# Modulation row 0 behind a third w2^T block, later sines behind the first norm, and the first MLP block among the last w2^T blocks

## The chip, the cores and the metric

The kernel runs on one core of a Trainium2 chip. The core has TensorE (PE in the profile; its weight loads are listed apart as PEld), VectorE (DVE), ScalarE (ACT), GpSimd (POOL) and SyncE (SP), which issues most of the DMA transfers. The metric is the device time of one execution in microseconds. Every number is a time on the chip or a line of a profile taken there.

## The reference, cut to what matters

The computation is one transformer-like block, forward and backward, in bf16: S = 2048 tokens, D = 1024 channels, F = 3584 hidden units. Six modulation rows come from one vector c.

```python
def _A_ref(x, w_r, w_i):                       # spectral filter over tokens and channels
    X = rfft2(x.astype(float32))
    return irfft2(X * (w_r + 1j * w_i), s=(S, D)).astype(bfloat16)

def _B_ref(x, w1, b1, w2, b2):                 # MLP with a norm of its own
    h = gelu(layernorm(x) @ w1 + b1)           # tanh approximation
    return h @ w2 + b2

mod = (silu(c) @ w_mod).reshape(1, 6, 1, 1024)
sa, ca, ga, sb, cb, gb = mod rows 0 .. 5
h = layernorm(x) * (1 + ca) + sa
x = x + ga * _A_ref(h, A_w_r, A_w_i)
h = layernorm(x) * (1 + cb) + sb
x = x + gb * _B_ref(h, B_w1, B_b1, B_w2, B_b2)
# returned: x, and the gradients of the weighted output with respect to
# A_x, A_w_r, A_w_i, B_w1, B_b1, B_w2, B_b2, c and w_mod, for a given grad_out
```

## The kernel before, in words

Tokens go in four chunks of 512 (index i, b or j), hidden units in 28 blocks of 128 (fc), modulation rows in halves of 512 columns. The Fourier transforms are matrix products with sine and cosine matrices that the kernel makes itself. The program is laid out at build time: a scheduler puts the instructions into one fixed list for each engine, by priority and by dependencies. Besides the data, three kinds of calls order it: `ordered()` chains matmuls behind the last one, `issue_after(x)` places what follows behind x in a list, and `behind(a, b)` places one instruction behind another. On the chip each engine works through its own list in order, and so does the queue of SP.

The parts that the change touches come in this order:

- **Start.** `start_load` issues the first transfers on SP, one behind the other: modulation weights (`w`), blocks of w2 transposed by the DMA (`t`, `load_w2t`, L344), chunks of grad_out (`g`) and of x (`x`). `mod_block(r, h)` computes half h of modulation row r in 8 matmuls (L280, out to `rows`, `sar` and others at L283). `pt_part` transposes grad_out (L386). `ph_part(fc, js)` computes block fc of ph = w2^T times the transposed gradient, 8 matmuls for each token chunk j (L371), copies the result out on DVE or ACT (L377) and stores it to `d_ph` (L379). `wt`, the tile for w2^T, holds two blocks `fg`, each of two fc, so a new block can only be loaded when the block two before it is used up.
- **Sine matrices.** `gen_mats` calls `trig` ten times. Each call makes index products on POOL (L460), masks them on DVE (L487) and takes the sine on ACT (L488). Calls 1 to 6 fill the matrices `smA` and `smB` of the token transform; calls 7 to 10 give `em`, the small matrices of the channel transform, which ACT then scales (L513) and POOL stores (`d_E`, L516).
- **Norm and fold of x.** For each chunk, statistics (`ln_dve` on DVE at L538 to L549, or `ln_mix`, half on DVE and half as squares on ACT, L548 to L556), a square root on ACT (L528), the normalisation on ACT (`norm_act`, L563), and then the scaling by 1 + row 1 and the even and odd parts over tokens and channels on DVE (`fold_tok`, `fold_d`, `fold_pair`; all recorded at L196, tile `fbuf`). Row 0 is folded alone (`sar`, `saf`) and added at the end.
- **Spectral core.** Its first matmuls are pu (L586 and L580), followed by pcs (L625), pv (L695, L711) and po (L793). Free `ph_part` matmuls (L371) stand between and behind them. `consume_fwd` takes each chunk of the result on DVE and ACT: unfolding, residual, two norms, and the store of the normed chunk `d_n3` (L898, called `d_n` in the profile).
- **MLP.** `load_w1` loads the seven blocks of w1 (L912). `z_block(b, g)` loads its part of ph (L964), computes z for token chunk b and w1 block g in 32 matmuls (pz, L970), and evaluates gelu and its derivative on ACT (L973, L980, L984, L986) and DVE. Before the first block of a chunk the normed chunk is loaded transposed (`n3Ta`, `n3Tb`, L955). `bo_pass` computes the output (pbo, L1027). `plan` is the written-out order of z blocks, remaining ph parts and output passes. The backward pass follows.

In `plan` the first z block stands ahead of the remaining halves of the last four ph blocks:

```python
plan = [("z", 0, 0)] + [("p", fc, 0) for fc in range(PH_KEEP, NFC)] + [("z", 0, 1), ("z", 0, 2), ("z", 0, 3)]
```

ACT evaluates sine, square root and sigmoid from tables, and loads another table (ACT_TABLE_LOAD) when its list goes from one to another.

Of the kernel before, what the change touches and what calls it, by code (L numbers as in the profile page):

```python
# [23 lines left out]
NFC = F // P  # L24
# [11 lines left out]
def kernel(  # L36
# [390 lines left out]
    for what in (("w", 5, 0), ("t", 0), ("w", 5, 1), ("g", 0), ("g", 1), ("x", 0), ("g", 2), ("g", 3),  # L427
                 ("w", 1, 0), ("w", 1, 1), ("x", 1), ("t", 1), ("x", 2), ("x", 3)):
        start_load(*what)
    for step in ((mod_block, 5, 0), (mod_block, 5, 1), (pt_part, 0, range(4), held), (gb_turn,), (pt_part, 0, range(4, 8)),  # L430
                 (pt_part, 1, range(4)), (ph_part, 0, (0,)), (pt_part, 1, range(4, 8)), (ph_part, 1, (0,)),
                 (pt_part, 2, range(4)), (ph_part, 0, (1,)), (pt_part, 2, range(4, 8)), (ph_part, 1, (1,)),
                 (pt_part, 3, range(4)), (ph_part, 0, (2,)), (pt_part, 3, range(4, 8)), (ph_part, 1, (2,)),
                 (mod_block, 1, 0), (mod_block, 1, 1), (ph_part, 0, (3,)), (ph_part, 1, (3,))):
# [42 lines left out]
    gcount = [0]  # L477

    def trig(dst, colv, rowv, nrow, width, modn, cosine):
# [3 lines left out]
        for r in range(nrow):  # L483
# [3 lines left out]
        nc.vector.tensor_scalar(out=idx[:, 0:n], in0=idx[:, 0:n], scalar1=modn - 1, scalar2=None, op0=ALU.bitwise_and)  # L487
        nc.scalar.activation(out=dst, in_=idx[:, 0:n].rearrange("p (r w) -> p r w", w=width), func=ACT.Sin,  # L488
                             bias=negpi[:], scale=2 * np.pi / modn)
# [341 lines left out]
    for h in range(2):  # L831
        mod_block(0, h)
# [17 lines left out]
    load_w2t(2)  # L850
    for fc in range(2, PH_EARLY):
        ph_part(fc, (0, 1, 2, 3))
        if fc % 2 == 1:
            load_w2t(fc // 2 + 2)
            if fc > 3:
                with tc.issue_after(last_pe[0].ins):
                    for r, h in late_mods[3 * (fc // 2 - 2):3 * (fc // 2 - 1)]:
                        mod_block(r, h)

    scaled = []  # L860
    for i in range(4):
        x4, fb = x4s[i], fbuf[:, i]
        if i == 0:
            with tc.issue_after(ev_v[1, 2].ins), tc.issue_after(ev_a[1, 7].ins):
                ln_dve(x4, 0, i)
                norm_act(fb, x4, 0, i)
        else:
            with tc.issue_after(ev_v[3, 6].ins if i == 1 else scaled[i - 2].ins), tc.issue_after(ev_a[3, 7].ins):
# [5 lines left out]
        if i % 2 == 0:  # L874
            fold_d(fb, fb, x4[:])
# [40 lines left out]
    for fc in range(PH_EARLY, NFC):  # L916
        if fc % 2 == 0 and fc > PH_EARLY + 2:
            load_w2t(fc // 2)
            load_w1((0, 2, 1, 4)[max(fc // 2 - 10, 0)])
        ph_part(fc, (0, 1, 2, 3) if fc < PH_KEEP else (0, 1))  # L920
# [30 lines left out]
    def z_block(b, g0, g1):  # L951
        n3T = n3Ts[b % 2]
        if g0 == 0:
            with tc.issue_after(w2ts[11].ins) if b == 0 else ExitStack():
                n3_in = nc.sync.dma_start_transpose(out=n3T[:], in_=d_n3[b * BW:(b + 1) * BW, :])  # L955
            if b == 0:
                for ins in w1_in[:2]:
                    behind(ins, n3_in)
        for g in range(g0, g1):
# [3 lines left out]
            with tc.issue_after(w2t_in[0].ins) if n < 2 else ExitStack():  # L963
                nc.sync.dma_start(out=ph, in_=d_ph_v[:, g * 4:(g + 1) * 4, b * BW:(b + 1) * BW])  # L964
# [98 lines left out]
    plan = [("z", 0, 0)] + [("p", fc, 0) for fc in range(PH_KEEP, NFC)] + [("z", 0, 1), ("z", 0, 2), ("z", 0, 3)]  # L1063
# [7 lines left out]
    for kind, b, g in plan:  # L1071
        if kind == "z":
            z_block(b, g, g + 1)
        elif kind == "p":
# [509 lines left out]
```

## Time and profile before

| | |
|---|---|
| runs | 1439.34, 1443.11, 1444.62 us; median 1443.11 |
| profiled execution | 1442.74 us, of which the span is 1441.0 |
| PE busy | 1382.4 us, 96% of the span |
| DVE busy | 1071.3 us, 74% |
| ACT busy | 743.2 us, 52% |
| POOL busy | 372.5 us, 26% |
| memory traffic | read 166.77 MB, written 115.92 MB, 196 GB/s over the span |

The page also cuts the span into 40 slices of 36 us. Each digit is the busy share in tenths; the third line is the clock that TensorE was granted, in tenths of full speed, and the last the share of the DMA engines:

```profile
PE   6799999979989999999999999999999999999998
DVE  5598889949889787787711588999488658998633
PEclk9799999989999999999999999999999999999999
DMA  9961564898877687697999479986689998667994
```

Slices 1 and 2 are the start with the modulation rows, slice 4 the end of the fold of x, slice 9 the change from the w2^T blocks to the MLP. A row of a timeline gives the start, the duration, the engine, the line, the instruction with its tiles and shapes, the number of instructions taken together, and in brackets the idle time of the engine before it and what ended that. A row of the waits gives microseconds in total, times, and the longest. In a row of windows the busy time of PE, PEld, DVE, ACT and POOL stands with the number of instructions, followed by the granted clock, the share of the DMA engines and GB/s.

### The profile page before, as it was taken

The numbers are of one execution on the slowest core, as the hardware profiler recorded it, in microseconds if no ns is written. First come the engines' busy times: TensorE is split into PE (matmuls) and PEld (weight loads), VectorE is DVE, ScalarE is ACT, GpSimd is POOL, SyncE is SP. The second block draws the span as 40 slices with busy tenths as digits, with TensorE's granted clock in tenths as the row PEclk, the third lists the DMA queues.
The fourth block names the chain that finished last, engine by engine and source line by source line (L and its number), as shares of the span: only waits on it lengthen the run. The fifth ranks groups of instructions, "written<-read, shape, count | busy, mean of one in ns | idle before, by whom it ended". The sixth has DMA issues, their size and how long they took to land. (4 is left out here: it accounts for less than half of the span.)

```text
span 1441.0 us, 18701 instructions
## 1 busy us (share of the span) xinstructions
PE 1382.4 (96%) x6963; PEld 664.6 (46%) x6963; DVE 1071.3 (74%) x1506; ACT 743.2 (52%) x1059; POOL 372.5 (26%) x479
## 2 busy tenths in 40 slices
PE   6799999979989999999999999999999999999998
PEld 3244566434434444444444444444544565444443
DVE  5598889949889787787711588999488658998633
ACT  5575667645887765666413583243532444433211
POOL 6210452400212122122211011112356431322323
PEclk9799999989999999999999999999999999999999
DMA  9961564898877687697999479986689998667994
GB/s 338 295 208 64 150 216 138 229 297 287 252 238 254 220 252 242 203 265 257 254 307 264 129 210 307 280 246 189 222 261 286 246 203 232 188 177 185 281 221 154
DMA packets 356689, 333.22 MB, mean 231 GB/s; under 512 B 207578, under 2 KB 297200, under 8 KB 356470
## 3 DMA queue, kind: packets, MB, share of 16 engines
q1 hardware_dynamic: 319110, 205.61, 54.6%
q0 software_dynamic: 37488, 126.42, 25.1%
q8 instruction: 54, 0.88, 0.3%
q14 instruction: 37, 0.30, 0.1%
HBM read 166.77 MB, written 115.92 MB: 196 GB/s over the span
## 5 line engine op out<-in xcount | busy, mean ns | idle before, releaser
L371 PE MATMUL pp<-gBoT,wt 128*128 128x512 bf16 x896 | 204.9, 388 | 13.4 <-DMA wt<-in_B_w_dram 8.4
L1127 PE MATMUL pg<-w1T,gzr 128*128 128x512 bf16 x896 | 196.1, 379 | 2.6 <-ACT gn3b L1142 1.7
L1478 PE MATMUL gw1acc<-gzh,n3n 128*128 128x512 bf16 x896 | 195.2, 379 | 0.6 <-DVE gwo L1267 0.6
L371 PEld LDWEIGHTS <-wt 128*128 128x128 bf16 x896 | 89.0, 100 | 120.9 <-issue 15.0
L970 PEld LDWEIGHTS <-w 128*128 128x128 bf16 x896 | 87.7, 98 | 112.2 <-issue 9.0
L1127 PEld LDWEIGHTS <-gzr 128*128 128x128 bf16 x896 | 86.5, 98 | 110.7 <-issue 7.9
L1478 PEld LDWEIGHTS <-n3n 128*128 128x128 bf16 x896 | 87.5, 98 | 104.9 <-issue 1.3
L970 PE MATMUL pz<-n3Ta,w 128*128 128x512 bf16 x448 | 100.5, 384 | 5.0 <-ACT gt L973 5.0
L970 PE MATMUL pz<-n3Tb,w 128*128 128x512 bf16 x448 | 99.0, 379 | 0.0
L196 DVE TENSOR_TENSOR ct<-ct 128x2048 bf16<-128x2048 bf16 x68 | 81.0, 1219 | 17.3 <-DMA d_n<-ct 16.3
L973 ACT ACTIVATE gt<-pz,b_col 128x512 bf16<-128x512 f32 x112 | 73.3, 684 | 38.9 <-PE pz L970 38.5
L1027 PEld LDWEIGHTS <-hhA 128*128 128x128 bf16 x608 | 59.0, 98 | 72.3 <-issue 2.1
L1260 PE MATMUL gw2acc<-gB,hhsA 128*128 128x512 bf16 x416 | 91.9, 379 | 0.0
L1482 ACT CAST gwo<-gw1acc 128x512 bf16<-128x512 f32 x49 | 28.6, 583 | 109.9 <-PE gw1acc L1478 102.8
L196 DVE TENSOR_TENSOR gt<-gt,gt 128x2048 bf16<-128x2048 bf16 x56 | 68.5, 1223 | 20.7 <-ACT gt L986 19.6
L984 ACT ACTIVATE gt<-gt 128x2048 bf16<-128x2048 bf16 x28 | 53.4, 1909 | 56.4 <-DVE gt L196 56.4
L1267 ACT CAST gwo<-gw2acc 128x512 bf16<-128x512 f32 x46 | 26.5, 583 | 97.3 <-PE gw2acc L1260 82.8
L377 ACT CAST pho<-pp 128x512 bf16<-128x512 f32 x53 | 30.6, 580 | 66.8 <-PE pp L371 66.7
L1260 PEld LDWEIGHTS <-hhsA 128*128 128x128 bf16 x416 | 40.7, 98 | 47.8
L980 ACT ACTIVATE gt<-gt 128x2048 bf16<-128x2048 bf16 x28 | 53.5, 1910 | 1.5 <-DVE w2sA L196 0.8
L1483 POOL DMA_DIRECT2D out_dram<-gwo x56 | 30.7, 549 | 90.3 <-ACT gwo L1482 54.1
L986 ACT ACTIVATE gt<-gt 128x2048 bf16<-128x2048 bf16 x28 | 53.4, 1909 | 0.4
(345 smaller groups left out, 2544.3 us busy)
## 6 DMA issues: line engine op xcount, KB each, us to landing
gzr<-d_gz SPq DMA_DIRECT2D x28, 512.0 KB, 6.4
wblk<-in_w_mod_dram SPq DMA_DIRECT2D x12, 1024.0 KB, 6.7
out_dram<-otl POOLq DMA_DIRECT2D x48, 256.0 KB, 4.4
out_dram<-gwo POOLq DMA_DIRECT2D x96, 128.0 KB, 4.2
d_ph<-pho POOLq DMA_DIRECT2D x21, 512.0 KB, 4.9
d_hh<-hhA POOLq DMA_DIRECT2D x19, 512.0 KB, 5.0
w<-in_B_w_dram SPq DMA_DIRECT2D x7, 1024.0 KB, 6.1
hhC<-d_ph SPq DMA_DIRECT2D x14, 512.0 KB, 3.5
```

The source lines that it names most:

```text
L196: return nc.vector.tensor_tensor(out=out, in0=a, in1=b, op=op)
L371: last_pe[0] = nc.tensor.matmul(pp[:], lhsT=wt[:, fg % 2, cch, k * P:(k + 1) * P], rhs=gBoT[j][:, cch, :], start=(cch == 0), stop=(cch == ...
L970: last_pe[0] = nc.tensor.matmul(pz[:], lhsT=w1s[g][:, cch, k * P:(k + 1) * P], rhs=n3T[:, cch, :], start=(cch == 0), stop=(cch == NDC - 1))
L973: z_in = nc.scalar.activation(out=zb[:, k, :], in_=pz[:], func=ACT.Identity, bias=b1_col[:, fc:fc + 1], scale=1.0)
L980: nc.scalar.activation(out=av, in_=zb, func=ACT.Square)
L984: nc.scalar.activation(out=sg, in_=bv, func=ACT.Sigmoid, scale=2.0 * GK)
L986: nc.scalar.activation(out=bv, in_=bv, func=ACT.Sigmoid, scale=-2.0 * GK)
L1027: last_pe[0] = nc.tensor.matmul(pbs[i][:], lhsT=hh[:, k, i * P:(i + 1) * P], rhs=wp[:, k, :], start=False, stop=(g == 6 and k == 3))
L1127: last_pg[0] = nc.tensor.matmul(pgs[i][:], lhsT=gzs[b, g][:, k, i * P:(i + 1) * P], rhs=w1Ts[g][:, k, h * KH:(h + 1) * KH], start=(g == 0 ...
L1260: nc.tensor.matmul(acc[:], lhsT=hh_of(fc)[:, t, :], rhs=gBs[t // 4][:, t % 4, h * KH:(h + 1) * KH], start=(t == 0), stop=(t == NT - 1))
L1478: nc.tensor.matmul(acc[:], lhsT=n3ns[t // 4][:, t % 4, cch * P:(cch + 1) * P], rhs=gz2[t // 8][:, t % 8, :], start=(t == 0), stop=(t == NT ...
L1483: nc.gpsimd.dma_start(out=out_4[cch * P:(cch + 1) * P, fg * 512:(fg + 1) * 512], in_=ob)
```

## The change

The change moves work and leaves the arithmetic alone.

1. At the start, x2 is loaded ahead of w2^T block 1. Both halves of row 0 are loaded through `start_load` and computed in the chained order, behind `ph_part(2)`, and w2^T block 2 is loaded behind them. Row 1 is computed ahead of the last five transposes of grad_out's fourth chunk. The late modulation rows are also placed behind the load of block 2.
2. From the fifth `trig` call on, the masks are placed behind the last copy of grad_out's transposes, and the sines behind the norm of x0. From the seventh call on, the masks also go behind the fold of x0. The statistics of x1 to x3 wait for x0's norm in the list, rather than for an earlier copy on ACT.
3. The w1 loads are spread as 0, 1, 1, 5 over the last four `load_w2t` calls in place of 0, 2, 1, 4. Only the first of them is placed behind the load of n3Ta; those from the third on are placed behind the first load of ph.
4. The loop over ph blocks ends at fc 25, and the first halves of fc 26 and 27 come behind the first z block (kind "q" in `plan`).

```diff
-                 ("w", 1, 0), ("w", 1, 1), ("x", 1), ("t", 1), ("x", 2), ("x", 3)):
+                 ("w", 1, 0), ("w", 1, 1), ("x", 1), ("x", 2), ("t", 1), ("x", 3)):
         start_load(*what)
...
-                 (pt_part, 3, range(4)), (ph_part, 0, (2,)), (pt_part, 3, range(4, 8)), (ph_part, 1, (2,)),
-                 (mod_block, 1, 0), (mod_block, 1, 1), (ph_part, 0, (3,)), (ph_part, 1, (3,))):
+                 (pt_part, 3, range(4)), (ph_part, 0, (2,)), (mod_block, 1, 0), (mod_block, 1, 1),
+                 (pt_part, 3, range(4, 8)), (ph_part, 1, (2,)), (ph_part, 0, (3,)), (ph_part, 1, (3,)),
+                 (ph_part, 2, (0, 1, 2, 3))):
...
-        nc.vector.tensor_scalar(out=idx[:, 0:n], in0=idx[:, 0:n], scalar1=modn - 1, scalar2=None, op0=ALU.bitwise_and)
-        nc.scalar.activation(out=dst, in_=idx[:, 0:n].rearrange("p (r w) -> p r w", w=width), func=ACT.Sin,
-                             bias=negpi[:], scale=2 * np.pi / modn)
+        late = gcount[0] > 4
+        with tc.issue_after(ev_v[3, 6].ins) if late else ExitStack():
+            masked = nc.vector.tensor_scalar(out=idx[:, 0:n], in0=idx[:, 0:n], scalar1=modn - 1, scalar2=None, op0=ALU.bitwise_and)
+        if gcount[0] > 6:
+            late_masks.append(masked)
+        sine = nc.scalar.activation(out=dst, in_=idx[:, 0:n].rearrange("p (r w) -> p r w", w=width), func=ACT.Sin,
+                                    bias=negpi[:], scale=2 * np.pi / modn)
+        if late:
+            late_sines.append(sine)
...
     for h in range(2):
-        mod_block(0, h)
+        start_load("w", 0, h)
+        with ordered():
+            last_pe[0] = mod_block(0, h, wm[0, h][:])
+    start_load("t", 2)
...
-    load_w2t(2)
-    for fc in range(2, PH_EARLY):
+    for fc in range(3, PH_EARLY):
         ph_part(fc, (0, 1, 2, 3))
...
-                with tc.issue_after(last_pe[0].ins):
+                with tc.issue_after(last_pe[0].ins), tc.issue_after(w2ts[2].ins):
...
                 norm_act(fb, x4, 0, i)
+            for ins in late_sines:
+                behind(ins, norm_in[0][3])
+            x0_norm = norm_in[0][3]
         else:
-            with tc.issue_after(ev_v[3, 6].ins if i == 1 else scaled[i - 2].ins), tc.issue_after(ev_a[3, 7].ins):
+            with tc.issue_after(ev_v[3, 6].ins if i == 1 else scaled[i - 2].ins), tc.issue_after(x0_norm.ins):
...
-            fold_d(fb, fb, x4[:])
+            folded = fold_d(fb, fb, x4[:])
+            for ins in late_masks if i == 0 else ():
+                behind(ins, folded)
...
-            load_w1((0, 2, 1, 4)[max(fc // 2 - 10, 0)])
-        ph_part(fc, (0, 1, 2, 3) if fc < PH_KEEP else (0, 1))
+            load_w1((0, 1, 1, 5)[max(fc // 2 - 10, 0)])
+        if fc < NFC - 2:
+            ph_part(fc, (0, 1, 2, 3) if fc < PH_KEEP else (0, 1))
...
-                for ins in w1_in[:2]:
-                    behind(ins, n3_in)
+                behind(w1_in[0], n3_in)
...
-                nc.sync.dma_start(out=ph, in_=d_ph_v[:, g * 4:(g + 1) * 4, b * BW:(b + 1) * BW])
+                ph_in = nc.sync.dma_start(out=ph, in_=d_ph_v[:, g * 4:(g + 1) * 4, b * BW:(b + 1) * BW])
+            for ins in w1_in[2:] if n == 0 else ():
+                behind(ins, ph_in)
...
-    plan = [("z", 0, 0)] + [("p", fc, 0) for fc in range(PH_KEEP, NFC)] + [("z", 0, 1), ("z", 0, 2), ("z", 0, 3)]
+    plan = [("z", 0, 0)] + [("q", fc, 0) for fc in range(NFC - 2, NFC)] + [("p", fc, 0) for fc in range(PH_KEEP, NFC)] + [("z", 0, 1), ("z", 0, 2), ("z", 0, 3)]
...
+        elif kind == "q":
+            with ordered():
+                ph_part(b, (0, 1))
```

2 lines of the change are left out of this document (1 added, 1 removed).

## The prediction

> **What bounds the kernel now.** I read the page's head first, then TensorE's waits, then its timeline with the queues beside it.
>
> ```profile
> span 1441.0 us, 18701 instructions
> PE 1382.4 (96%) x6963; PEld 664.6 (46%) x6963; DVE 1071.3 (74%) x1506; ACT 743.2 (52%) x1059; POOL 372.5 (26%) x479
> ```
>
> TensorE (PE) works 96% of the span, so 58.6 us in all can be won by taking waits away. The waits list, TensorE only (what waited, for what; us in total, times, longest), says which of them are large:
>
> ```profile
> PE pm L280 <- DMA wblk<-in_w_mod_dram: 14.8, 4, 4.4
> PE pp L371 <- DMA wt<-in_B_w_dram: 8.4, 1, 8.4
> ```
>
> Both sit where the change works. The timeline of TensorE (start, duration, instruction, count, idle time before it with its releaser) places them:
>
> ```profile
> 43.44 3.62 PE L280 MATMUL pm<-wblk,u_b 128*128 128x512 bf16 x16
> 46.89 3.62 PE L371 MATMUL pp<-gBoT,wt 128*128 128x512 bf16 x16
> 54.96 3.60 PE L280 MATMUL pm<-wblk,u_b 128*128 128x512 bf16 x8 [4.45 <-DMA wblk<-in_w_mod_dram]
> 62.54 3.59 PE L280 MATMUL pm<-wblk,u_b 128*128 128x512 bf16 x8 [3.98 <-DMA wblk<-in_w_mod_dram]
> ...
> 134.32 0.83 PE L586 MATMUL pu<-smA,fbuf 128*128 128x256 bf16 x6 [2.30 <-DVE fbuf L196]
> ...
> 234.58 75.49 PE L371 MATMUL pp<-gBoT,wt 128*128 128x512 bf16 x349
> 318.44 3.59 PE L371 MATMUL pp<-gBoT,wt 128*128 128x512 bf16 x8 [8.38 <-DMA wt<-in_B_w_dram]
> 325.98 14.25 PE L371 MATMUL pp<-gBoT,wt 128*128 128x512 bf16 x56 [3.94 <-DVE phr L377]
> ...
> 411.43 8.75 PE L970 MATMUL pz<-n3Ta,w 128*128 128x512 bf16 x32 [4.58 <-ACT gt L973]
> ```
>
> Three places: the two halves of modulation row 0 (4.45 + 3.98 us, and each half takes 3.6 us for 8 matmuls where 16 took 3.62); the fold of x before the spectral work (2.30); the change-over to the MLP (8.38 + 3.94, later 4.58). By stretches (length, then busy us and count of PE, PEld, DVE, ACT, POOL; granted clock; DMA share; GB/s):
>
> ```profile
> 55.00:59.00 4.00, 3.56 (x8) 0.99 (x8) 0.41 (x1) 3.85 (x8) 0.00 (x0) 0.50 1.04 420
> 59.00:63.00 4.00, 0.46 (x2) 0.19 (x3) 0.28 (x1) 0.00 (x0) 0.00 (x0) 0.50 1.04 389
> ...
> 300.00:311.00 11.00, 10.07 (x47) 4.35 (x45) 3.16 (x8) 10.32 (x12) 1.07 (x2) 1.00 1.17 301
> ...
> 340.00:411.00 71.00, 66.43 (x310) 29.76 (x308) 58.76 (x77) 60.87 (x62) 12.13 (x15) 1.00 0.72 236
> ```
>
> The slow matmuls stand at a granted clock of 0.50 behind a wait of about 4 us. The Trainium skill, page "TensorE: Matmul & The Clock Gate", says in its part on the clock gate that an idle array falls back to half clock; these rows agree.
>
> **The change, part by part.**
>
> *Row 0 behind a third w2^T block.* Thirty-two matmuls of L371 (w2^T block fc 2) move ahead of row 0: 32 x 3.62/16 = 7.2 us of work into the 8.4 us of waits. The second half of row 0 is not earlier by itself; it can only gain what leaves its way. The 1 MB store of the inverse matrices does:
>
> ```profile
> 52.05 0.57 POOL L516 DMA_DIRECT2D d_E<-em  x1 [0.30 <-POOL em L515]
> ```
>
> It now follows later sines. At 389 GB/s 1.05 MB is 2.7 us, so that half starts between 59.9 and 62.5; I take 60.5, and half clock again after a wait of some 3 us. Row 0 then ends near 64.1 rather than 66.1, with 7 us of matmuls already done: TensorE is 9 to 9.5 us ahead. The block needs its own transfer, now behind x2:
>
> ```profile
> 29.78 10.50 SPq L344 DMA_TRANSPOSE wt<-in_B_w_dram  x1
> 40.32 1.95 SPq L143 DMA_DIRECT2D x<-in_A_x_dram  x2
> ...
> 300.91 14.17 SPq L344 DMA_TRANSPOSE wt<-in_B_w_dram  x1
> ```
>
> It is issued 1.95 us later on SP's queue. The block issued at 300.91 took 17.5 us to its use at 318.44, and I know of none slower; 31.7 + 17.5 = 49.2, before TensorE is through at 50.5. So nothing, up to 2.5 us if x2's half megabyte stretches it.
>
> *Sines behind the first norm of x.* ACT and DVE, timelines and (third row) ACT's groups by form:
>
> ```profile
> 46.59 1.28 ACT L528 ACT_TABLE_LOAD   x1
> 47.89 0.30 ACT L528 ACTIVATE mv<-mv,eps_c 128x4 f32<-128x4 f32 x1
> ...
> 70.61 0.59 ACT L377 CAST pho<-pp 128x512 bf16<-128x512 f32 x1 [11.76 <-PE pp L371]
> ...
> 82.77 1.24 ACT L563 ACTIVATE fbuf<-x,stats 128x1024 bf16<-128x1024 bf16 x1
> ```
> ```profile
> L488 ACT ACTIVATE em<-gidx,negpi 128x512 bf16<-128x512 int32 x4 | 2.8, 714 | 0.5 <-DVE gidx L487 0.5
> ```
> ```profile
> 84.10 2.28 DVE L196 TENSOR_TENSOR fbuf<-fbuf,rows 128x4096 bf16<-128x4096 bf16 x1
> 86.30 0.69 DVE L548 BATCH_NORM_STATS2 st<-x 128x6 f32<-128x512 bf16 x1
> ...
> 133.57 0.69 DVE L196 TENSOR_TENSOR fbuf<-fbuf,sb_saf 128x1024 bf16<-128x1024 bf16 x1
> ...
> 324.09 1.23 DVE L196 TENSOR_TENSOR ct<-ct 128x2048 bf16<-128x2048 bf16 x1 [16.31 <-DMA d_n<-ct]
> ```
>
> x0 is scaled and folded early, but the end of the fold (134.26) hangs on x1: its norm ends at 84.0, its scaling starts at 84.10, and 50.2 us of DVE work for x1 to x3 follow with little idle time. After the change the four em sines (2.8 us) and two further table loads (sqrt, sine, sqrt in place of one: 2 x 1.28) stand ahead of x1's norm on ACT, and on DVE a small copy that waits for row 0's matmuls holds the em masks and x1's statistics. ACT's hole of 11.76 us covers most of that: I follow the chain to 84.8, and the fold's end to +1 us (call it d). From below, -1: part of x2's statistics (0.69 us each, as at 86.30) can be done in DVE's free time before x1. From above, +2.5: both loads and half the sines uncovered. Without the hole it would be 2.8 + 2.6 = 5.4, near +6.
>
> In TensorE's order as built 49 more matmuls of L371 stand ahead of the first spectral matmul that needs the fold. 49 x 0.226 = 11 us against 9.5 won: TensorE arrives there as before and waits 2 to 3 us, as before 2.30. So the win is not time yet: it is 46 to 49 finished matmuls, taken from the run of 349 at 234.58. That run would be through some 10 us earlier, and then TensorE waits for the next w2^T block.
>
> *The MLP's start.* So the transfers decide. SP's queue (the row of 300.91, shown above, belongs at the first gap), and the issues of 1 MB (KB each, us to landing) in the same stretch:
>
> ```profile
> 273.29 0.40 SPq L898 DMA_DIRECT2D d_n<-ct  x1
> 282.47 3.09 SPq L344 DMA_TRANSPOSE wt<-in_B_w_dram  x1
> 285.66 13.84 SPq L955 DMA_TRANSPOSE n3Ta<-d_n  x1
> 299.69 1.13 SPq L912 DMA_DIRECT2D w<-in_B_w_dram  x2
> ...
> 315.27 0.44 SPq L912 DMA_DIRECT2D w<-in_B_w_dram  x1
> 315.80 1.34 SPq L898 DMA_DIRECT2D d_n<-ct  x1
> ```
> ```profile
> w<-in_B_w_dram SPq DMA_DIRECT2D x6, 1024.0 KB, 6.1
> ...
> d_x<-xt POOLq DMA_DIRECT2D x2, 1024.0 KB, 7.4
> ```
>
> The block issued at 282.47 waited for TensorE to free its buffer, and the transpose n3Ta stood behind it in the queue. With TensorE 46 x 75.49/349 = 9.9 us ahead, less d, that block goes out right behind the store of the first normed chunk (273.29), and n3Ta waits only for that store: 6.1 to 7.4 us, 279.4 to 280.7. That is 5.0 to 6.3 us earlier than 285.66; I take 5.6. Zero is the other end, if transposes are limited by their transfer and not by their issue. One w1 block less stands ahead of the next w2^T block: 0.56 us of issue and, at 301 GB/s, 1.05 MB = 3.5 us of transfer. So that block, and the second normed chunk's store behind it, come 5.6 + 0.56 + 3.5 - d (1.0) = 8.7 us earlier. The three w1 blocks that now follow a load of ph cost nothing as long as they are used tens of us later; each 1 MB that came late would show as a wait of up to 6.1 us at its block.
>
> Who uses this: DVE waits 16.31 us for that store and frees at 324.09; ACT's and DVE's gelu work then sets the pace to 411.43. TensorE, if it alone decided, has 92.99 - 3.94 - 4.58 = 84.5 us of work from 318.44 to 411.43: from 309.7 it would be there at 394.2 and would wait. So the end of the lead-in moves by DVE's 8.7 us. The 3.94 us wait of TensorE goes with it and is no gain of its own. Against it: the first MLP block now comes among the last w2^T blocks, and ACT, between sqrt and gelu's sigmoid, gets two more table loads, 2 x 1.28 = 2.6 us. ACT is idle 71.00 - 60.87 = 10.1 us of that stretch; so 0 to 2.6, I take 1.3. From the first output matmuls on, the order is the old one.
>
> The Trainium skill, page "ScalarE: Activation LUTs", section "What ACT_TABLE_LOAD costs", adds a drain of about 1.38 us to a load of 1.28. The rows at 46.59 and 47.89 agree on the load and show no drain: the square root starts 0.02 us behind it.
>
> *Sum:* -8.7 + 1.3 = -7.4 us on the profiled execution's 1442.74 (span 1441.0 and 1.74 around it): 1435.3. The median of the runs, 1443.11, lies 0.4 us above that execution. No change is within 0.5%, 7.2 us: 1435.9 to 1450.3.
>
> **The rivals.**
>
> *B, more.* The waits at the MLP's start fall away wholly, ACT's 10.1 us absorb the loads, the fold is 1 us early: -6.3 - 0.56 - 3.5 - 1 = -11.4 and some of the 4.58 us: 1429. For it: TensorE has the 84.5 us of work ready. Against: DVE and ACT are 83 to 86% busy there.
>
> *C, given back.* The fold of x comes some 5 us later than I take it, or n3Ta is no earlier because transposes are bound by transfer: -3.5 - 0.56 + 1.0 + 1.3 = -1.8, or -8.7 + 5 + 1.3 = -2.4: 1440.5. This is also the rival that the change does nothing: row 0's wait turns into one for the fold. For it: a block takes 17.5 us from issue to use, far more than its issue.
>
> *By the page's table switch.* Two switches of 2.66 us, none of it covered: -8.7 + 5.3 = -3.4, 1439.3. In terms of this kernel it is an ACT that loses 2.6 us twice between gelu pieces while TensorE waits on it at L970. Only the loads themselves are in the rows.
>
> *D, slower.* In the new order DVE evacuates the first tile of that next w2^T block before the unfolding that now waits 16.31 us. If the block lands no earlier than 318.44, DVE begins its unfolding where it did, behind an evacuation, and the first MLP block's gelu work (four evacuations, three passes of ACT, seven of DVE) is pushed in front of the second chunk's norms. Then +2.6 to 5.2 us from ACT, and a wait for the last w2^T block before the rest: 1446 to 1452, say 1449. It decides from where the block lands 3 us or more after 318.44. For it: n3Ta and two w2^T blocks in flight at once at a DMA share of 1.17.
>
> **How the numbers follow.** A, as summed, 0.46, own range 1430 to 1439 (0.33 of it faster); B 0.13; C 0.20; the page's switch 0.04; D 0.17. Faster 0.33 + 0.13 = 0.46; within 0.5%, 0.13 + 0.20 + 0.04 = 0.37; slower 0.17. The range leaves out half of D and a third of B: 1428 to 1448.
>
> **What the profile of the changed kernel would show.** Row 0: no wait of 4.45 us, L371 x32 before it, one wait near 3 us. The fold: first needed L586 matmul at 134 to 137, with a wait of 2 to 3 us. The long L371 run: about 303 matmuls rather than 349 before the wait. SP: n3Ta near 280, the next w2^T block near 296. DVE's unfolding free near 315.4 rather than 324.09. The gelu wait at L970 near 404 where it was 411.43, then equal distances to the end. The prediction is wrong if the fold ends past 138, if the wait for wt ends at 318 again, or if ACT's waits at L970 grow by over 5 us.

## The result, and the profile after

The changed kernel takes 1453.51 us (median of 16 runs, 1443.69 to 1466.49) against 1443.03 us for the kernel before (16 runs): a ratio of 1.0084, 95% interval 1.0056 to 1.0112. It is slower by some 10.5 us, where 7.4 us faster was forecast. Its times spread over 23 us, more than those of the kernel before (1432.44 to 1449.73); why is part of the answer. The profiled execution took 1464.85 us, at the slow end. Its page and its list of TensorE's waits:

```profile
span 1463.1 us, 18570 instructions
PE 1372.6 (94%) x6838; PEld 662.9 (45%) x6963; DVE 1071.9 (73%) x1503; ACT 750.9 (51%) x1066; POOL 370.7 (25%) x479
```
```profile
PE pp L371 <- DMA wt<-in_B_w_dram: 40.3, 3, 20.0
PE pz L986 <- ACT gt L989: 12.2, 4, 6.0
PE pm L280 <- DMA wblk<-in_w_mod_dram: 6.5, 3, 3.9
```

The waits for the modulation weights have more than halved (14.8 before), as meant. The waits for w2^T blocks went from 8.4 to 40.3 us. TensorE's timeline tells where (start, duration, instruction, count, idle time before it and its releaser):

```profile
44.04 12.25 PE L371 MATMUL pp<-gBoT,wt 128*128 128x512 bf16 x55 [0.56 <-DVE gBoT L396]
56.12 1.89 PE L280 MATMUL pm<-wblk,u_b 128*128 128x512 bf16 x8
58.34 1.89 PE L280 MATMUL pm<-wblk,u_b 128*128 128x512 bf16 x7 [0.32 <-DMA wblk<-in_w_mod_dram]
...
68.74 13.99 PE L371 MATMUL pp<-gBoT,wt 128*128 128x512 bf16 x62 [1.13 <-DMA wt<-in_B_w_dram]
...
107.86 16.43 PE L371 MATMUL pp<-gBoT,wt 128*128 128x512 bf16 x63 [19.96 <-DMA wt<-in_B_w_dram]
...
153.59 0.83 PE L593 MATMUL pu<-smA,fbuf 128*128 128x256 bf16 x6 [0.95 <-DVE fbuf L196]
...
253.02 65.34 PE L371 MATMUL pp<-gBoT,wt 128*128 128x512 bf16 x296
337.55 9.03 PE L371 MATMUL pp<-gBoT,wt 128*128 128x512 bf16 x32 [19.19 <-DMA wt<-in_B_w_dram]
```

Row 0 is through at 60.2 us (66.1 before). Then two waits of about 20 us stand where there was none and where there was one of 8.38. The first is for w2^T block 3 (fc 6 and 7): the fold of x, first needed at 134.32 before, is first needed at 153.59. DVE's timeline shows how a wait for w2^T gets into the fold:

```profile
90.02 1.21 DVE L196 TENSOR_TENSOR x<-fbuf 128x2048 bf16<-128x2048 bf16 x1
111.49 0.69 DVE L377 CAST pho<-pp 128x512 bf16<-128x512 f32 x1 [20.27 <-PE pp L371]
112.10 1.22 DVE L196 TENSOR_TENSOR x<-fbuf 128x2048 bf16<-128x2048 bf16 x1
```

The copy of block 3's first result out of PSUM (L377) stands in DVE's list in the middle of the fold of x1 (L196). DVE works its list in order, so it stands still for 20.27 us with fold work behind it that lacks nothing. The windows of that stretch, after and then before (length; busy us and count of PE, PEld, DVE, ACT, POOL; granted clock, DMA share, GB/s):

```profile
82.00:88.00 6.00, 5.85 (x27) 2.46 (x26) 6.00 (x7) 3.28 (x8) 0.53 (x1) 1.00 0.83 60
88.00:108.00 20.00, 0.14 (x1) 0.13 (x2) 3.23 (x5) 4.03 (x4) 0.00 (x0) 0.61 1.16 146
```
```profile
88.00:108.00 20.00, 20.00 (x95) 9.05 (x93) 19.88 (x33) 14.18 (x22) 1.07 (x2) 1.00 0.70 226
```

From 88 on TensorE stands still and DVE and ACT have little to do. The DMA engines are busier than before (1.16 against 0.70), and they move less: 60 GB/s in the 6 us ahead of the hole, then 146 against 226. What was in flight, from the queues of SP and POOL:

```profile
57.44 11.36 SPq L272 DMA_DIRECT2D wblk<-in_w_mod_dram  x3
70.80 2.18 SPq L612 DMA_DIRECT2D ws<-in_A_w_r_dram  x1
...
74.51 30.67 SPq L344 DMA_TRANSPOSE wt<-in_B_w_dram  x2
...
292.13 0.40 SPq L912 DMA_DIRECT2D d_n<-ct  x1
292.64 5.11 SPq L344 DMA_TRANSPOSE wt<-in_B_w_dram  x1
297.86 22.26 SPq L970 DMA_TRANSPOSE n3Ta<-d_n  x1
320.34 1.17 SPq L926 DMA_DIRECT2D w<-in_B_w_dram  x1
321.60 13.89 SPq L344 DMA_TRANSPOSE wt<-in_B_w_dram  x1
```
```profile
77.90 0.63 POOL L523 DMA_DIRECT2D d_E<-em  x1 [0.30 <-POOL em L522]
```

Ahead of block 3 (issued at 74.51) stand three late modulation weights of 1 MB each, and 3.4 us behind it, on POOL's queue, the 1 MB store of the inverse matrices (d_E), which the later sines brought there from 52.05. From issue to use block 3 took 107.86 - 74.51 = 33.35 us.

### The profile page after: what moved, and what is told of

The parts are those of the page before. It is cut to its first block, busy times and chain, and to the rows that moved or that the text cites. A ratio compares the mean times of both kernels' runs of the same rounds, so it can differ in the third digit from the quotient of the medians.

```text
span 1463.1 us, 18570 instructions
## 1 busy us (share of the span) xinstructions
PE 1372.6 (94%) x6838; PEld 662.9 (45%) x6963; DVE 1071.9 (73%) x1503; ACT 750.9 (51%) x1066; POOL 370.7 (25%) x479
## 5 line engine op out<-in xcount | busy, mean ns | idle before, releaser
L371 PE MATMUL pp<-gBoT,wt 128*128 128x512 bf16 x873 | 201.1, 386 | 44.9 <-DMA wt<-in_B_w_dram 40.3
L1501 ACT CAST gwo<-gw1acc 128x512 bf16<-128x512 f32 x49 | 28.6, 583 | 110.4 <-PE gw1acc L1497 99.9
L196 DVE TENSOR_TENSOR ct<-ct 128x2048 bf16<-128x2048 bf16 x68 | 81.0, 1217 | 4.2 <-DMA d_n<-ct 3.2
L196 DVE TENSOR_TENSOR gt<-gt,gt 128x2048 bf16<-128x2048 bf16 x56 | 68.4, 1224 | 16.1 <-ACT gt L1002 14.9
L377 ACT CAST pho<-pp 128x512 bf16<-128x512 f32 x61 | 35.2, 587 | 80.2 <-PE pp L371 78.5
```

Of the source, the lines that this page charges most:

```text
L196: return nc.vector.tensor_tensor(out=out, in0=a, in1=b, op=op)
L371: last_pe[0] = nc.tensor.matmul(pp[:], lhsT=wt[:, fg % 2, cch, k * P:(k + 1) * P], rhs=gBoT[j][:, cch, :], start=(cch == 0), stop=(cch == ...
```

## The experiments

The runs of one letter, and e1 with f1 and f2, were measured together with the kernel before. Each ratio is to the kernel before of its own group; between groups the ratios can be compared, the times in microseconds only roughly (the kernel before has medians of 1441.1 to 1443.5). Two tables hold what was read from the profiles, one execution each; the runs follow.

*Block 3.* Queue mark: how long SP took to issue the first ws load. I read 0.35 us as room in SP's queue, and more as a queue in which the loads ahead are not through yet. Then the issue of block 3, the issue of the d_E store, TensorE's first use of the block and its wait, and the first needed pu matmul (for b3 the end of the fold). In b4 and c2 block 3's matmuls stand in one unbroken run with the others. In b1, b2 and e1 row 0 ended late (65.9 to 68.0), which moves the fold by itself.

| run | queue mark | block 3 | d_E | use | wait | fold needed |
|---|---|---|---|---|---|---|
| after | 2.18 | 74.51 | 77.90 | 107.86 | 19.96 | 153.59 |
| a1 | 1.83 | 71.28 | 75.03 | 97.02 | 11.82 | 142.58 |
| c1 | 1.58 | 68.46 | 72.03 | 95.53 | 10.54 | 141.75 |
| b1 | 0.35 | 74.45 | 79.27 | 92.06 | none | 140.28 |
| b2 | 0.35 | 76.61 | 81.43 | 104.42 | none for wt | 148.04 |
| a2 | 1.74 | 69.38 | 73.20 | 103.14 | 18.18 | 148.90 |
| a4 | 1.64 | 82.27 | 51.81 | 102.80 | 5.02 | 143.65 |
| b3 | 1.88 | 69.65 | 73.35 | 102.00 | 16.94 | 129.70 |
| f2 | 1.75 | 69.48 | 73.30 | 96.78 | 11.55 | 142.62 |
| d1 | 0.35 | 67.34 | 72.14 | 87.39 | 2.28 | 132.47 |
| d2 | 1.27 | 68.58 | 101.86 | 86.44 | 1.03 | 131.77 |
| e1 | 0.35 | 75.19 | 108.21 | 92.80 | none | 140.69 |
| b4 | 0.35 | 67.76 | 72.58 | in the run | none | 135.17 |
| c2 | 0.35 | 67.52 | 72.31 | in the run | none | 134.83 |
| before | 0.35 | 80.96 | 52.05 | 99.76 | none | 134.32 |
| f1 | 0.35 | 76.34 | 79.09 | 95.14 | none | 129.69 |
| d3 | 0.35 | 77.14 | 50.86 | 95.94 | none | 130.51 |

*The whole time in four pieces.* Start of the long run of w2^T matmuls; from there to the moment DVE begins to unfold the second chunk; from there to the first matmul on n3Tb; the rest.

| run | run starts | to DVE's unfolding | to n3Tb | rest | span |
|---|---|---|---|---|---|
| before | 234.58 | 89.5 | 99.4 | 1017.5 | 1441.0 |
| after | 253.02 | 92.1 | 102.9 | 1015.2 | 1463.1 |
| a1 | 241.86 | 90.5 | 102.4 | 1015.3 | 1450.0 |
| a2 | 248.03 | 94.1 | 99.2 | 1013.5 | 1454.7 |
| a3 | 234.96 | 89.1 | 99.5 | 1015.4 | 1439.0 |
| c3 | 236.05 | 84.9 | 99.8 | 1014.7 | 1435.5 |
| c4 | 232.53 | 91.9 | 100.1 | 1014.1 | 1438.6 |
| b4 | 233.71 | 90.5 | 102.4 | 1015.6 | 1442.3 |
| c2 | 233.36 | 88.6 | 101.5 | 1013.6 | 1437.0 |
| d2 | 230.96 | 87.8 | 102.7 | 1013.1 | 1434.5 |
| e1 | 239.83 | 83.2 | 103.7 | 1013.6 | 1440.4 |
| f1 | 230.51 | 88.4 | 99.9 | 1017.1 | 1435.9 |
| d3 | 230.87 | 81.5 | 99.4 | 1014.3 | 1426.1 |

### The two halves of the change, and the sines

a1 is the changed kernel again. a2 keeps parts 1 and 2 and undoes the lead-in of the MLP (the w1 spread, the order behind ph, the kind "q"); a3 is the reverse; a4 undoes part 2 alone.

```diff
 a2
-            load_w1((0, 1, 1, 5)[max(fc // 2 - 10, 0)])
+            load_w1((0, 2, 1, 4)[max(fc // 2 - 10, 0)])
 ...
-    plan = [("z", 0, 0)] + [("q", fc, 0) for fc in range(NFC - 2, NFC)] + ...
+    plan = [("z", 0, 0)] + ...
 a4
-        late = gcount[0] > 4
 ...
-            for ins in late_sines:
-                behind(ins, norm_in[0][3])
```

> The changed kernel once more, as the base of the others. Theory L (the w2^T block for fc 6 and 7 lands late; behind its first matmuls stand copies out of PSUM in DVE's and ACT's lists, ahead of the fold of x): TensorE waits at L371 for wt near 90 to 108, by 8 to 20 us, DVE and ACT have a hole of nearly the same length, the first needed L593 matmul comes 6 to 19 us after 134.3, and the time varies with that wait. Rival S (the sines and table loads behind the first norm make the fold late): a late fold without a DVE hole behind a PE release. Time 1449 to 1465 by both.

> The start of the changed kernel (its parts 1 and 2) with the old MLP lead-in (parts 3 and 4 undone). Theory L: the wait for wt near 90 to 108 stays, and nearly all of the loss: 1448 to 1455, ratio to before 1.004 to 1.009. Rival M (the first z block among the w2^T blocks and two more table loads are the loss): 1436 to 1444, ratio 0.995 to 1.001.

> The old start with the new MLP lead-in (parts 3 and 4 alone). Theory L: within 4 us of before, 1439 to 1447, since TensorE isn't ahead there and the two table loads are covered or nearly. Rival M: 1449 to 1455, and waits at L970/L986 for ACT grow by 8 us or more.

> The changed kernel with its part 2 undone: sines, masks and statistics as before, row 0 behind the third w2^T block and the new MLP lead-in kept. SP's order of transfers is that of the changed kernel. Theory L: the wait for wt of 8 to 20 us stays, 1448 to 1456. Rival S: the wait or the hole of DVE goes, 1436 to 1444; the store of the inverse matrices is early again, so if it was what delayed the block, the wait falls below 4 us.

Measured: a1 1456.45 us (ratio 1.0107, 1.0081 to 1.0132); a2 1458.27 (1.0134, 1.009 to 1.0177); a3 1436.52 (0.996, 0.9928 to 0.9991); a4 1450.16 (1.0043, 1.0018 to 1.0067). The start carries the whole loss, and the lead-in alone is faster (a2 came out slower than either of its expected ranges, a3 faster); a3's and c3's profiles do not agree on where (c3 has it ahead of DVE's unfolding, a3 in the rest). a1's profile has the same stall in a smaller size; DVE's hole and TensorE's wait again go together:

```profile
97.02 16.26 PE L371 MATMUL pp<-gBoT,wt 128*128 128x512 bf16 x64 [11.82 <-DMA wt<-in_B_w_dram]
...
142.58 0.83 PE L593 MATMUL pu<-smA,fbuf 128*128 128x256 bf16 x6 [0.95 <-DVE fbuf L196]
```
```profile
100.66 0.69 DVE L377 CAST pho<-pp 128x512 bf16<-128x512 f32 x1 [10.84 <-PE pp L371]
```

In a4 the store is back at 51.81, now beside block 2, and it is block 2 that is late: issued at 50.17, used at 75.83, 25.7 us, with a wait of 6.71. Block 2 had the 2 MB of row 0's loads ahead of it and the store 1.64 us behind it. Block 3 then goes out at 82.27, with a full queue but no store beside it, and takes 20.5 us, of which TensorE waits 5.02; the fold is late (143.65) by holes of 9.53 and 6.65 us in DVE's list, one for each block.

### Does the wait cost through TensorE, or through the lists behind it?

b3 places block 3's copies out of PSUM behind the fold of x in their lists. b1, and c1 with the same kernel, were meant to hold block 4 back from block 3; the edit ordered instructions of different engines, which changed no engine's list, so both are further executions of the changed kernel. b2 places the last three late modulation weights behind block 3.

```diff
 b3
-                nc.any.tensor_copy(out=ov, in_=pv)
+                cp = nc.any.tensor_copy(out=ov, in_=pv)
+            if fc in (6, 7):
+                held_cp.append(cp)
 ...
+    for cp in held_cp:
+        behind(cp, fold_in)
 b2
-                with tc.issue_after(last_pe[0].ins), tc.issue_after(w2ts[2].ins):
+                with tc.issue_after(last_pe[0].ins), tc.issue_after(w2ts[3].ins):
 b1, c1
+            with tc.issue_after(last_pe[0].ins):
+                load_w2t(4)
```

> The changed kernel with w2^T block 4 (for fc 8 and 9) issued only behind the first tile of fc 6, so that block 3 is alone among the transposes in flight, as in the kernel before. Everything ahead of block 3 in the queue stays. If two transposes in flight are what makes block 3 late: it lands 16 to 20 us after its issue near 70, the wait for wt near 88 falls from 12 to 20 us to under 5, fold's end near 134 to 137, time 1437 to 1446. If what stands ahead of it in the queue (three modulation blocks of 1 MB) makes it late: the wait stays at 10 us or more, 1450 to 1458.

> The kernel of b1 once more, for a second profile: its times fell into two groups, 1443 to 1444 and 1452 to 1470, and the profiled execution was of the first. If the second group is the same stall: a wait of 8 us or more for wt or for a modulation block between 80 and 110 with a DVE hole of its length, and a time above 1450. If it lies elsewhere: no such wait, and a fold that ends before 137.

> The changed kernel with the three late modulation blocks (rows 2 and half of 3) loaded behind w2^T block 3 rather than ahead of it; block 4 follows them as before. If the 3 MB ahead of it make block 3 late: no wait for wt above 3 us at fc 6, instead a wait of 3 to 9 us for the modulation blocks near 83, time 1442 to 1450. If two transposes in flight are the cause, the three blocks between them also part them, so that no wait for wt is expected either; only b1 tells these two apart.

> The changed kernel with the copies out of PSUM of fc 6 and 7 placed behind the last instruction of the fold of x, the transfers as in the changed kernel. Theory L says that the late block costs through the lists of DVE and ACT: so the wait for wt of 10 to 20 us stays, but DVE has no hole of that length, and the fold ends at 122 to 130 instead of 142 to 154; TensorE has to wait for the copies and pays for it behind the fold, so the whole time is 1444 to 1454. If the fold is late on its own (sines, loads, statistics): it ends at 138 or later here too.

Measured: b3 1444.07 us (1.0012, 0.9984 to 1.0041). TensorE waits as long as in a1 and after, and longer, but the fold is not held (the profile puts the end of the first wait down to a DVE statistic, st, that these matmuls don't read; by its place it is the wait for block 3):

```profile
102.00 8.49 PE L371 MATMUL pp<-gBoT,wt 128*128 128x512 bf16 x32 [16.94 <-DVE st L557]
115.06 5.30 PE L371 MATMUL pp<-gBoT,wt 128*128 128x512 bf16 x16 [4.57 <-ACT pho L377]
130.36 6.19 PE L371 MATMUL pp<-gBoT,wt 128*128 128x512 bf16 x16 [10.00 <-DVE pho L377]
```
```profile
129.01 0.69 DVE L196 TENSOR_TENSOR fbuf<-fbuf,sb_saf 128x1024 bf16<-128x1024 bf16 x1
```

The fold ends at 129.70 although TensorE stands still for 31 us around it, and most of the loss is gained back. So the price runs through the lists of DVE and ACT (the copies of both were held), not through TensorE's lost time. b1: 1452.7 us (1.0042, 1.0006 to 1.0077), four of its ten times at 1442.7 to 1444.4 and six at 1452.4 to 1470.2; its profile, one of the four, has no stall and a queue mark of 0.35 us. c1: 1453.06 us, with the stall. So there are four profiles of the changed kernel's lists: three with the stall, at 1451.75 (a1), 1453.06 and 1464.85 us, and b1 without it, at 1444.37. b2: 1449.56 us (1.003, 0.9999 to 1.0061); block 3 is in time, but now TensorE waits 5.62 us for the modulation weights that stand behind it, with DVE's copy waiting in its turn (7.21), and row 0 ended late in that profile (68.0).

### Which transfers make block 3 late

b4 computes all late rows behind fc 7 and loads them behind block 3, so that the 3 MB no longer stand ahead of it; it holds b1's edit too, and block 4 goes out behind those loads. d1, and f2 with the same kernel, hold block 4 behind the second three modulation weights. d2 leaves the 3 MB ahead and moves the d_E store alone, behind the ph stores of fc 6 and 7. f1 goes the other way: in the kernel before it puts that store right behind block 3's issue, with no loads left in the queue (the last two modulation weights went out at 61.01, 15 us ahead of block 3, and the queue mark is 0.35).

```diff
 b4
-            if fc > 3:
-                with tc.issue_after(last_pe[0].ins), tc.issue_after(w2ts[2].ins):
-                    for r, h in late_mods[3 * (fc // 2 - 2):3 * (fc // 2 - 1)]:
+            if fc > 5:
+                for r, h in late_mods:
+                    with tc.issue_after(last_pe[0].ins), tc.issue_after(w2ts[3].ins):
 d1, f2
+    behind(w2ts[4], mod_in[0])
 d2 (ph_st: the last store of ph, fc 7)
+    behind(de_st[0], ph_st[0])
 f1 (kernel before; ph_st[3]: the store of fc 3)
+    behind(de_st[0], ph_st[3])
```

> As b1, and the late modulation rows 2 to 4 all behind fc 7, their loads behind w2^T block 3: nothing large stands ahead of block 3, and nothing transposes beside it. Theory L: wait for wt at fc 6 under 4 us whichever of its two causes counts, fold's end near 131 to 136, TensorE 40 or more matmuls ahead as forecast, time 1432 to 1441. If it is still above 1446, the early start itself (the order of the sines and norms) costs time.

> The changed kernel with w2^T block 4 behind the loads of the second three late modulation blocks in SP's list, which wait for TensorE's first late rows: so block 4 can't be issued before block 3 has been alone for some 15 us. The 3 MB ahead of block 3 and the store of the inverse matrices beside it stay. If two transposes in flight make block 3 late: wait for wt at fc 6 under 5 us, all times below 1450, median 1441 to 1447. If what stands ahead of block 3 does: the wait stays at 8 us or more in most executions, median 1450 to 1458, spread over 15 us.

> The kernel of d1 (block 4 held back, store and queue as in the changed kernel) once more, for a second profile: its times went from 1439.6 to 1456.0, and the execution profiled was the fastest. If its slow executions have the same stall: a wait for wt of 6 us or more at fc 6, DVE idle about as long, time above 1448; then block 4 is no condition for it.

> The changed kernel with the 1 MB store of the inverse matrices behind the stores of ph of fc 6 and 7 on GpSimd's list, so that it no longer runs beside block 3; queue and transposes as in the changed kernel. If that store, moved there by the late sines, makes block 3 late: no wait above 4 us, median 1441 to 1447. If not: as the changed kernel, waits of 0 to 20 us, median 1450 to 1458.

> The kernel before with nothing changed but the 1 MB store of the inverse matrices, placed behind the store of ph of fc 3 on GpSimd's list, near 82, just behind the issue of w2^T block 3. If such a store beside a block in transposition is enough to make it late: a wait for wt of 4 to 15 us near 100, a fold later by as much, 1444 to 1456. If it needs the 3 MB ahead in the queue as well: no such wait; the store leaves the way of row 0, whose second half then starts 1 to 2.6 us earlier than 62.5, and 1439 to 1443.

Measured: b4 1441.32 us (0.9992, 0.9962 to 1.0023); d1 1447.84 (1.0043, 1.0012 to 1.0073); f2 1452.77; d2 1438.9 (0.9982, 0.9953 to 1.0011); f1 1438.35 (0.9983, 0.9958 to 1.0009). Every time of d2 (1433.78 to 1442.54) is below every time of the changed kernel. d2 on SP, POOL and TensorE:

```profile
65.77 1.27 SPq L614 DMA_DIRECT2D ws<-in_A_w_r_dram  x1
...
68.58 17.18 SPq L344 DMA_TRANSPOSE wt<-in_B_w_dram  x2
```
```profile
101.86 0.53 POOL L525 DMA_DIRECT2D d_E<-em  x1
```
```profile
86.44 13.99 PE L371 MATMUL pp<-gBoT,wt 128*128 128x512 bf16 x64 [1.03 <-DMA wt<-in_B_w_dram]
...
131.77 0.83 PE L595 MATMUL pu<-smA,fbuf 128*128 128x256 bf16 x6 [0.95 <-DVE fbuf L196]
```

b4 keeps the store (72.58) and takes the loads away; f1 has the store 2.75 us behind the block, without the loads:

```profile
67.76 2.56 SPq L344 DMA_TRANSPOSE wt<-in_B_w_dram  x1
70.36 12.02 SPq L272 DMA_DIRECT2D wblk<-in_w_mod_dram  x3
```
```profile
76.34 15.63 SPq L344 DMA_TRANSPOSE wt<-in_B_w_dram  x2
```
```profile
79.09 0.53 POOL L518 DMA_DIRECT2D d_E<-em  x1
```

Without the store (d2) or with no loads left in the queue ahead (b4, c2, f1) there is no stall: the two together make it. d2's queue mark (1.27) is lower than those of the stalled executions, but a4 has 1.64 without a store beside block 3 and took 20.5 us; and d2's ten times speak for more than its one profile. Block 4 is no condition: f2 holds it back and stalls. The first table sorts the executions the same way. All six with a full queue at the ws loads (1.58 to 2.18 us) and the store behind wait 10.5 to 20 us. The ones with the store and a mark of 0.35, b1 and d1 among them, wait 0 to 2.3 us. How far behind block 3 the store was issued differs as well, 3.4 to 3.8 us in the six and 4.8 in b1, b2, b4, c2 and d1; but f1 has 2.75 and no stall, so a short distance alone does not do it. All this fits the spread of the changed kernel's times: whether the modulation loads are through by then differs from execution to execution. Four profiles make that likely, no more.

What the DMA engines do in the stall stays open. The store is held up with the block: from issue to landing it took 27.4 us in a2 and 25.5 in f2, against 7.4 in f1 and 6.6 in d2, where nothing stalls (17.5 in d1). The Trainium skill, page "DMA: Bandwidth & Descriptors", section "Queues, rings and completion order", says that each DMA engine alternates between the queues that have work, a packet at a time. As an estimate, a mere sharing would cost about the store's own transfer, 1 MB at the 389 GB/s of row 0's stretch, 2.7 us. f1, where nothing waits for the block, does not speak against so little; the 10 to 20 us of the stalled executions are more than that.

### The lead-in of the MLP

c4 adds to the kernel before a further 1 MB store on POOL's queue at the lead-in (a copy of chunk 0 into d_gx1, on which the output does not depend), to see whether the amount in flight sets the time. c2 is b4 with the first w1 block behind the next-to-last w2^T block; d3 is a3 with that edit, on the old start; c3 is a3 again. e1 is d2 with the same w1 edit.

```diff
 c4
+        if i == 0:
+            nc.gpsimd.dma_start(out=chunk_rows(d_gx1, i), in_=tmp)
 c2, d3, e1
-            load_w1((0, 1, 1, 5)[max(fc // 2 - 10, 0)])
+            load_w1((0, 0, 2, 5)[max(fc // 2 - 10, 0)])
 ...
-                behind(w1_in[0], n3_in)
+                behind(w1_in[0], w2ts[12])
```

> The kernel before with the first normed chunk stored a second time, 1 MB more on GpSimd's queue, into a buffer that is overwritten later; nothing waits for it. If the MLP's start is held by the amount of transfers: the wait for wt that ended at 318.4 ends 2.5 to 4.5 us later relative to the long L371 run, DVE's unfolding frees as much later than 324.1, and the kernel is 2 to 5 us slower, 1444 to 1449. If it is held by the latency of a chain of transposes: within 1 us of before in all three.

> b4 (whose fold is on time and whose TensorE is ahead) with the first w1 block, 1 MB, loaded behind the next-to-last w2^T block rather than ahead of it. If the transfers between the store of the first normed chunk and that block are what holds TensorE: the wait for wt, which ended 83.0 us after the start of the long L371 run in b4, ends 2.5 to 4.5 us nearer to it, and the kernel is 1 to 4 us faster than b4, 1437 to 1441. If the time of the transposes is fixed by something else: 83 us again and no gain.

> The kernel of a3 (the old start with the new MLP lead-in) again, with more rounds: 1434 to 1442, ratio to before 0.994 to 1.000. It is faster than both kernels if the interval stays under 1.

> The old start, the new MLP lead-in, and the first w1 block too behind the next-to-last w2^T block (the edit of c2 on the kernel of a3). If both gains add: 1430 to 1436, ratio to before 0.990 to 0.996, and the wait for wt after the long L371 run ends 3 to 4 us earlier than 83.7 us after that run's start. If not: 1434 to 1440.

> The changed kernel with the edit of d2 (store of the inverse matrices behind ph of fc 6 and 7) and that of c2 (first w1 block behind the next-to-last w2^T block). If the stall and the queue ahead of that block were the two things that ate the early start: no wait above 4 us at fc 6, DVE's unfolding free 82 to 86 us after the start of the long L371 run, 1430 to 1436. If the early start brings nothing at the MLP's start even so: 1436 to 1441, and d3 (1430.8), which has no early start, stays the fastest.

Measured: c4 1440.36 us (0.9986, 0.9959 to 1.0013); c2 1438.35 (0.9986, 0.996 to 1.0011); c3 1434.36 (0.9962, 0.993 to 0.9994); d3 1430.83 (0.992, 0.9891 to 0.9949); e1 1442.64 (1.002, 0.9993 to 1.0048). A megabyte more on the other queue costs no time (c4): TensorE's wait ended 84.3 us after the start of the run, 83.9 before, though DVE's unfolding began 2.4 us later in that profile. With a megabyte less ahead in SP's own queue, TensorE's wait ends at 79.1 us in c2 where b4 has 83.0, and DVE's unfolding begins earlier: at 88.6 us in c2 where b4 has 90.5, at 83.2 in e1 where d2 has 87.8, and at 81.5 in d3 where a3 and c3 have 89.1 and 84.9. These are single profiles, and a3 and c3, the same kernel, differ by 4.2 us. d3, the new lead-in with that edit on the old start, is 0.8% below the kernel before, and by the two ratios (0.992 and 1.0084) 1.6% below the changed one. Its queue, TensorE and DVE:

```profile
281.09 10.23 SPq L956 DMA_TRANSPOSE n3Ta<-d_n  x1
292.57 7.56 SPq L344 DMA_TRANSPOSE wt<-in_B_w_dram  x1
```
```profile
230.87 77.22 PE L371 MATMUL pp<-gBoT,wt 128*128 128x512 bf16 x357
314.27 7.46 PE L371 MATMUL pp<-gBoT,wt 128*128 128x512 bf16 x24 [6.18 <-DVE phr L377]
```
```profile
312.39 1.22 DVE L196 TENSOR_TENSOR ct<-ct 128x2048 bf16<-128x2048 bf16 x1 [8.30 <-DMA d_n<-ct]
```

TensorE no longer waits for wt there, and DVE waits 8.30 us for the second chunk's store instead of 16.31.

e1 was to join both mends with the early start. It is no faster than d2, and slower than d3, which shares everything with it but the start and the store's place. In its profile block 3 does not stall, but block 1 came late, row 0 ended at 66.6, the fold was first needed at 140.69, and from DVE's unfolding to n3Tb it takes 103.7 us. So the stall is not the only way in which the new start goes late. What the w1 edit gains by itself is not shown: by the ratios 0.4% beside c3 (0.992 against 0.9962, intervals that overlap), 0.1% beside b4 (0.9986 against 0.9992), and nothing beside d2 (1.002 against 0.9982).

## Why the prediction was wrong, point by point

*Row 0.* Right in kind, too cautious in size: the wait of 4.45 us is gone, 55 or 56 matmuls precede it, it ended at 60.2 instead of the forecast 64.1, and at full clock (1.89 us for 8 matmuls) since the waits were under 1 us. With 7.2 us of matmuls done and 5.9 us earlier, TensorE was 13 us ahead, not 9 to 9.5. b1, b2 and e1, with row 0 ending at 65.9 to 68.0, show that this differs by execution: block 1, whose transfer the prediction had at 17.5 us, took 21.3 to 22.5 us to its use there, and TensorE waited 2.6 to 3.3 us for it.

*The next w2^T blocks: the step that failed.* The prediction took 17.5 us from issue to use as the worst case ("I know of none slower"), applied it to block 1 (fc 2 and 3), and costed the blocks behind it at nothing. The trace of the kernel before has a slower one: its own block 1, issued at 29.78, took 18.9 us to land. In the profile after, block 1 came in time and block 2 nearly (1.13 us of wait), but block 3 took 33.35 us, and 25.7 to 33.8 in the six stalled executions of the new start. In part 2 it counted the d_E store only as a gain where it leaves, never as a cost where it arrives. The forecast fold at 134 to 137 became 141.7 to 153.6 in the stalled executions whose lists were not altered; the bound it gave itself, "past 138", is what happened (in b1, b2 and e1 too, by the late row 0).

*The fold itself.* d was forecast as +1, from -1 to +2.5. Where no stall hides it, the fold is first needed at 131.8 to 135.2 if row 0 ends near 58.5 (d1, d2, b4, c2), and at 140.3 and 140.7 if it ends late (b1, e1); with the old start it is 129.7 to 137.2. Counting from the end of row 0 (L211, TensorE's next instruction, marks it) removes that difference. The scaling of x1 starts 21.3 to 21.8 us later in these six, and DVE waits some 3 us for ACT's norm there; with the old start it is 17.5 to 18.1 us in before, f1, d3, a3, c3 and c4, without that wait. In d2, row 0 ends at 58.5, in e1 at 66.5:

```profile
80.28 2.29 DVE L196 TENSOR_TENSOR fbuf<-fbuf,rows 128x4096 bf16<-128x4096 bf16 x1 [3.16 <-ACT fbuf L572]
```
```profile
87.83 2.29 DVE L196 TENSOR_TENSOR fbuf<-fbuf,rows 128x4096 bf16<-128x4096 bf16 x1 [2.78 <-ACT fbuf L572]
```

The forecast chain, 64.1 to 84.8, was 20.7 us and nearly right. So the new order on ACT, with the em sines and a table load between row 0 and that norm, costs the fold 3 to 4 us, and only an early row 0 hides it; that the sines are the cause is read from ACT's list and was not tried without a stall (a4 has one). What was unforeseen is that the fold's own list holds copies that wait for TensorE. The hole adds its whole length: d2's 73.25 us from row 0's end (58.52) to the fold, plus the hole, gives 153.7 for the profile after (60.15 + 73.25 + 20.27) and 142.8 for a1 (58.75 + 73.25 + 10.84), where 153.59 and 142.58 were measured.

*The MLP's start: nothing came of 8.7 us.* The carried matmuls are there (303 in a1 before the wait, as forecast), and n3Ta is issued earlier counted from the start of the run: 297.86 - 253.02 = 44.8 us after it, 51.1 before. But its issue took 22.26 us instead of 13.84 (24.42 in a1; 20.8 to 24.4 in all seven profiles with the new start in the second table, 10.0 to 14.1 in the six with the old one), so the next w2^T block went out at 68.6 us instead of 66.3. TensorE's wait for it ended 84.5 us after the start of the run (83.0 in a1) against 83.9, and DVE's unfolding began 2.6 us later (1.0 in a1) instead of 8.7 earlier. The prediction had named this end, "Zero is the other end, if transposes are limited by their transfer and not by their issue", and rival C rested on it. c4 shows that a megabyte more in flight does not set it; c2 and d3 speak for the order in SP's queue.

*Table loads.* +1.3 was forecast. In a3, c3 and d3, which have both extra loads, the stretch from the unfolding to n3Tb takes 99.4 to 99.8 us, as before (99.4): they cost nothing. With the new start it takes 101.5 to 103.7 us, in a2 (new start, old lead-in) 99.2. The price belongs to the combination. ACT's list differs there: in a1 it puts the norm's four pieces between the square root and the sigmoid, 8.4 us from load to load, and in d3 the loads follow each other in 1.6 us.

```profile
366.82 1.28 ACT L535 ACT_TABLE_LOAD   x1
...
375.25 1.28 ACT L1002 ACT_TABLE_LOAD   x1
```
```profile
347.55 1.28 ACT L528 ACT_TABLE_LOAD   x1
...
349.17 1.28 ACT L988 ACT_TABLE_LOAD   x1
```

That this order is the cause was not tried by itself.

*The sum.* a1, at 1451.75 us near the changed kernel's median, stands against the kernel before as +7.3 (the start of the run, moved by the stall), +1.0 (DVE's unfolding), +3.0 (the new lead-in's list), -2.2 (the rest) = +9.0 us on the span; the medians differ by 10.5. The forecast terms were 0, -8.7, +1.3. The slower rival D gave 1446 to 1452, near the measured time, but for a late unfolding at the MLP's start and 2.6 to 5.2 us more on ACT; these two are +1.0 and +3.0 of a1's 9.0 us, so that it comes near is in part luck. Of the rivals only C had a later fold, by 5 us, and only as a smaller gain; none had +7.3 at the start. The forecast would have missed without the stall as well: d2 is at 0.9982 of the kernel before, 1440.4 us on 1443.03, where 7.4 us faster is 0.9949, and its profile has -1.7 us at DVE's unfolding and +3.3 for the new lead-in's list. That is rival C's time (1440.5), for the second of its two reasons, an n3Ta that is there no earlier.

## What to carry to other kernels

A transfer that is moved out of one load's way lands beside another: for each one moved, list which loads it will share the queues with, and how long after their issue they are needed. Where an engine with a fixed list carries both filler work and the chain that sets the time, a late load of the filler stops the chain by its whole delay, so place the filler's copies behind the chain (b3 got back most of 10 us by that alone). A head start is worth what the next wait lets through: before counting it, follow the queue that sets the next start, and take out of that queue what can go behind (d3 gained 0.8% by the lead-in and one w1 load).

## What the runs showed of the hardware

Block 3, a transposing load of 0.5 MB, took 17.6 to 20.5 us from issue to use in b1, d2, d1, the kernel before and a4. It took 25.7 to 33.8 us when modulation loads of 3 MB had gone out ahead of it, by the queue mark were not all through, and a 1 MB store was issued beside it on another queue 3.4 to 3.8 us later; in the profile after, the DMA engines were busy meanwhile (0.83 to 1.16) and moved 60 to 146 GB/s, and the store itself took 25 to 27 us to land in a2 and f2. Either condition alone showed no such delay (the loads in d2 and a4, the store in f1, b1, b4 and d1). Between executions of one program the stall came and went (c1 has it, b1 has not), and b1's times fall into two groups 8 us apart. A further megabyte on POOL's queue cost no time (c4), while with one less in SP's queue ahead of a transposing load TensorE's wait for that load ended 3.8 us earlier (c2 against b4).
